# Memory update as a PSUM sum of its own, and long sums with 32-row shares from the first logits step on

## The chip, the cores and the metric

Every run used one core of a Trainium2 chip. The metric is device time in microseconds of one execution, taken from outside the profile. The profiled span (first to last instruction) is some 1.8 us shorter than the time of the same execution.

## The reference

`x` is 2048 x 1024. After a layer norm, two branches are added to the input:

```python
x = A_x
xn = _layernorm(x, axis=-1)
return x + _A_ref(xn, A_wq, A_wk, A_wv, A_wo, A_beta) + _B_ref(xn, B_w1, B_b1, B_w2, B_b2)

# A: 32 heads of 32, four segments of 512 tokens, causal inside a segment, and a memory over the segments
#    a_dot = softmax(q k' * scale + mask) v;  a_mem = (phi(q) M) / (phi(q) z + 1e-6)
#    o = g * a_mem + (1 - g) * a_dot;  then M += phi(k)' v, z += sum phi(k)
# B: token MLP: layer norm once more, gelu(h' w1 + b1) w2 + b2, with 2048 -> 3584 -> 2048 over the tokens
```

## The kernel before

The first MLP (h and w1) runs first, to about 200 us, and leaves `gT` (28 chunks of 128 rows). Everything else is interleaved after it by a list scheduler inside the program, which carries its own clock: attention is the fixed part, and the second MLP (`gT` times w2) with the output projection is "fill", put wherever attention would let TensorE wait. The scheduler is run when the program is built; on the chip the order is fixed.

Some words that come up often: PSUM is the memory that TensorE writes its results to, here in eight banks. A "sum" is a row of matmuls that add up in one bank. An "evacuation" is the copy by ScalarE or VectorE that empties a bank, after which the bank can be given to another sum. "Weighing" is the product of the softmax weights with v.

Attention comes in units (a group of four heads in one segment, 32 units). 46 logits steps feed them. A step has seven jobs in seven PSUM banks, of the eight: one 32-row group of TensorE has one job, the other three have two. So in the second half of a step one row group stands idle. A "long sum" of fill uses that: it leaves out its 28th chunk as a full matmul and does it as four shares of 32 rows, one in each of four steps.

```python
        def second(bs, some):                       # second half of a logits step
            if n >= fill.PLAIN and fill.L.sliced():
                fill.L.cut(rs)                      # the share, in row group rs, the one with a single job
            mms(bs, some)
```

The fill has two streams of weights, N (short sums, buffers `w2n`) and L (long sums, `w2l`, its share's slice in `w2s`):

```python
    PLAIN = 12                                      # the first 12 steps stand outside the scheme
    def __init__(self, k):
        rest = [(c, half, False, 0) for c in range(12, 16) for half in range(2)]
        long = []
        for j in range(3):
            g = [(c, half, True) for c in range(4 * j, 4 * j + 4) for half in range(2)]
            long += [x + (1,) for x in g[:3]]       # True: 8 matmuls of output projection in the same sum
            rest += [x + (0,) for x in g[3:]]
    ...
    def ready(self, t):                             # may the next logits step be placed?
        L, N, n = self.L, self.N, t.stage - 1
        if n < self.PLAIN:
            return N.open() and N.left() >= self.KEEP
        return L.i == self.want(n) and L.open() and not N.open()
```

The memory update sits in the last weighing of a unit and shares its bank:

```python
            if upd:                                 # in weigh(u, 3): pk' vA into columns of the same bank
                for c in range(4):
                    fw.mm(self.ps[:, b, 2 * GW:3 * GW], self.pk[u % 3][:, c, :],
                          vA[:, c, hl:hl + 4, :].rearrange("p h x -> p (h x)"), start=(c == 0), stop=(c == 3))
        ...                                         # ScalarE or VectorE: ost <- bank
        if upd:                                     # VectorE: memory <- bank, which only then is free
            fl.op({"dve": (lambda e, b: e.tensor_tensor(m32, m32, self.ps[:, b, 2 * GW:3 * GW], op=ALU.add), 283, 320)},
                  [R_o, self.R_MZ32[g]], [self.R_MZ32[g]], box=box, give=True, prio=0)
```

The softmax here doesn't subtract the row's maximum and nothing guards it: scores larger than these inputs give would overflow.

Of the kernel before, what the change touches and what calls it, by code (L numbers as in the profile page):

```python
# [7 lines left out]
ALU = mybir.AluOpType  # L8
# [7 lines left out]
N_SEG = 4  # L16
# [349 lines left out]
class _Flow:  # L366


    LOOK = 5
    MARGIN = 120  # L370
    MARGIN_STEP = 110
    PART = 160

# [61 lines left out]
    def next(self):  # L435
        fw, best = self.fw, None
        for t in self.avail:
            if t.gate is not None and not t.gate():
                continue
            reads = t.reads if t.box is None else t.reads + [self.R_bank[t.box["b"]]]  # L440
            r = fw.ready(reads, t.writes)
            for e, (fn, ns, busy) in t.engs.items():
                s = max(r, fw.now[e])
                key = (s, t.prio, t.n, s + ns)
                if best is None or key < best[0]:
                    best = (key, t, e, reads)
        return best
# [136 lines left out]
class _Kernel:  # L584
# [95 lines left out]
    def over_early(self):  # L680
# [5 lines left out]
        self.wkr = [e.take(f"wk{i}", [P, N_DCH, P], BF16) for i in range(2)]  # L686
        self.w2r = [e.take(f"w2n{i}", [P, 6, P], BF16) for i in range(4)]
        self.w2l = [e.take(f"w2l{i}", [P, 6, P], BF16) for i in range(3)]
        self.w2s = [e.take(f"w2s{i}", [P, P], BF16) for i in range(2)]
# [6 lines left out]
        self.R_wk = [Res(f"wk{i}", wait) for i in range(2)]  # L696
        self.R_w2 = [Res(f"w2n{i}", wait) for i in range(4)]
        self.R_w2l = [Res(f"w2l{i}", wait) for i in range(3)]
        self.R_w2s = [Res(f"w2s{i}", wait) for i in range(2)]
# [329 lines left out]
    def evac(self, dst, R_dst, box, view=lambda x: x):  # L1029
        self.flow.op({"act": (lambda e, b: e.activation(dst, view(self.bank(b)), ACT.Copy), 600, 540),  # L1030
                      "dve": (lambda e, b: e.tensor_copy(dst, view(self.bank(b))), 690, 727)},  # L1031
                     [], [R_dst], box=box, give=True, prio=0)
# [69 lines left out]
    def step(self, items):  # L1102
# [45 lines left out]
        for i, (r, blocks, slot, masks) in enumerate(items):  # L1148
            fl.op({"act": (lambda e, b, slot=slot: e.activation(pT[:, slot, :], self.bank(b), ACT.Exp, scale=SCALE),  # L1149
                           620, 488)}, [], [R[slot]], box=box[i], give=True)  # L1150
            v = pT[:, slot, :].rearrange("p (j q) -> p j q", q=P)
            if len(masks) > 1:
                ap, pat = v[:, masks[0]:masks[1] + 1:masks[1] - masks[0], :], [[0, 2], [1, P]]
            else:
                ap, pat = v[:, masks[0], :], [[1, P]]
            ns = 180 + 115 * len(masks)
            fl.op({"pool": (lambda e, ap=ap, pat=pat: e.affine_select(ap, ap, pattern=pat, compare_op=ALU.is_ge,  # L1157
                                                                      fill=0.0, base=0, channel_multiplier=-1),
                            ns, ns + 30)}, [R[slot]], [R[slot]])

    def weigh(self, u, qb):
# [5 lines left out]
        vA, R_vA = self.vA[i], self.R_vA[i]  # L1167
        upd = qb == 3 and s < N_SEG - 1
        where = {}
        for r in range(4):  # L1170
            for kb in range(qb + 1):
                slot, col = self.slot_of[u, r, kb]
                where[r, kb] = slot, col + (qb - kb) * P
        reads = [self.R_pT[slot] for slot in sorted({x[0] for x in where.values()})]
        reads += R_vA if upd else R_vA[0:qb + 1]
        if s:
            reads += [self.R_pqT[k], self.R_MZbf[g]]
        if upd:
            reads += [self.R_pk[u % 3]]

        def mms(b):
            fw = self.fw
            for r in range(4):
                for kb in range(qb + 1):
                    slot, col = where[r, kb]
                    fw.mm(self.ps[:, b, VW * r:VW * r + VW], self.pT[:, slot, col:col + P], vA[:, kb, hl + r, :],
                          start=(kb == 0), stop=(kb == qb))
            if s:
                fw.mm(self.ps[:, b, GW:2 * GW], self.pqT[k][:, qb * P:(qb + 1) * P], self.MZbf[:, g, :],
                      start=True, stop=True)  # L1190
            if upd:
                for c in range(4):
                    fw.mm(self.ps[:, b, 2 * GW:3 * GW], self.pk[u % 3][:, c, :],
                          vA[:, c, hl:hl + 4, :].rearrange("p h x -> p (h x)"), start=(c == 0), stop=(c == 3))

# [4 lines left out]
               "act": (lambda e, b: e.activation(dst, self.ps[:, b, 0:n * VW], ACT.Copy), 175 + n * 27, 140 + n * 27)},  # L1200
              [], [self.R_ost[o][qb]], box=box, give=not upd, prio=0)
        if upd:
            R_o = self.R_ost[o][qb]
            m32, mbf = self.MZ32[:, g, :], self.MZbf[:, g, :]
            dg = self.diag[:].rearrange("p r x -> p (r x)")
            if s == 0:
                fl.op({"dve": (lambda e, b: e.tensor_copy(m32, self.ps[:, b, 2 * GW:3 * GW]), 283, 320)},
                      [R_o], [self.R_MZ32[g]], box=box, give=True, prio=0)
            else:
                fl.op({"dve": (lambda e, b: e.tensor_tensor(m32, m32, self.ps[:, b, 2 * GW:3 * GW], op=ALU.add), 283, 320)},  # L1210
                      [R_o, self.R_MZ32[g]], [self.R_MZ32[g]], box=box, give=True, prio=0)
            fl.op({"dve": (lambda e: e.tensor_tensor(mbf, m32, dg, op=ALU.mult), 296, 330)},
                  [self.R_MZ32[g], self.R_diag], [self.R_MZbf[g]], prio=2)

# [44 lines left out]
    def attention_and_out(self):  # L1259
# [24 lines left out]
        for i, items in enumerate(steps):  # L1284
            fl.stage = i + 1
            self.step(items)
            while True:
# [4 lines left out]
                elif u < N_UNIT and last[u] <= i:  # L1292
                    self.proj_v(u)
                    for qb in range(4):
                        self.weigh(u, qb)
                    self.combine(u)
                    for slot in [x for x, us in self.users.items() if u in us]:
# [7 lines left out]
        goals = [0, 0]  # L1305
        knots = [(0, 0)] + [(last[8 * s + 7] + 2, 216 + 285 * s) for s in range(3)]
        knots += [(len(steps) - 1, self.fill.total - self.RESERVE), (len(steps), self.fill.total - 3)]
        for i in range(1, len(steps) + 1):
# [5 lines left out]
    def tail(self):  # L1314
# [37 lines left out]
        for x in pieces[5:]:  # L1352
            part(x, 0, 8)


# [117 lines left out]
class _Fill:  # L1473
    KEEP = 5
    PLAIN = 12
    SOON = 700

    def __init__(self, k):
        self.k = k
        self.closed = []  # L1480
        rest = [(c, half, False, 0) for c in range(12, 16) for half in range(2)]
        long = []
        for j in range(3):
# [3 lines left out]
        long[-1] = long[-1][:3] + (0,)  # L1487
        self.L = _Stream(k, self, long, "L", k.w2l, k.R_w2l, 2, [3])
        self.N = _Stream(k, self, rest, "N", k.w2r, k.R_w2, 3, [0, 1, 2])
        self.streams = [self.L, self.N]  # L1490
# [109 lines left out]
```

## Time and profile before

| | before |
|---|---|
| time, median of the runs beside the changed kernel | 692.03 us (691.76 to 692.76, 6 runs) |
| profiled span | 690.2 us |
| matmul records / weight loads | 4765 / 4846 |
| ScalarE, VectorE, GpSimd busy | 45%, 33%, 22% |

TensorE is the path, and the prediction shows by which lines. Two habits of reading are needed. Busy spans of matmuls overlap, so work is counted by start-to-start distances. And where matmul records are missing (81 here), the weight loads are complete and give the count.

I use one account for all kernels. A profile is split into the time to the first value projection (start and first MLP), the stretch from there to the start of the last matmul, and the end. The stretch is fixed work, counted matmul by matmul as in the prediction, and what is left of it: waits. Some 0.5 us of every figure for waits is reading error (46 steps by 0.01).

### The profile page before, as it was taken

To read this page: it belongs to the slowest core of one execution; us is meant where nothing else is said; L and a number is where in the kernel's file an instruction comes from. 1 tells how busy PE (TensorE), PEld (TensorE's weight loads), DVE (VectorE), ACT (ScalarE), POOL (GpSimd) and SP (SyncE) were. 2 spreads that over 40 slices of the span, in tenths; PEclk is the share of its full clock that TensorE was granted. 3 is DMA by queue.
4 is the path that set the end of the run, shared out by engine and by line. 5 is a ranking of instruction groups with operands and counts; after the bars stand their busy time and mean duration, and the time that the engine had idled before them with its cause. 6 is when DMAs were issued, how large, how long until landed. Compare 5 with 4: busy or idle time off the path is not lost.

```text
span 690.2 us, 11956 instructions
## 1 busy us (share of the span) xinstructions
PE 680.5 (99%) x4765; PEld 328.6 (48%) x4846; DVE 226.8 (33%) x500; ACT 313.5 (45%) x616; POOL 153.2 (22%) x379
## 2 busy tenths in 40 slices
PE   9999999999999999999999999999999999999998
PEld 3444444444444544544454444544545544454544
DVE  6731100000002323333453461633534534341524
ACT  7431111111136566564655462735754643644540
POOL 5820000000001233223223131312331331312330
PEclk9999999999999999999999999999999999999999
DMA  8367666325026558766556556465565456446334
GB/s 307 121 183 181 154 156 211 91 61 145 1 103 154 133 135 167 142 142 154 132 121 145 123 123 150 103 151 121 126 149 114 104 119 159 106 111 127 86 85 137
DMA packets 274960, 92.03 MB, mean 133 GB/s; under 512 B 233434, under 2 KB 271322, under 8 KB 274906
## 3 DMA queue, kind: packets, MB, share of 16 engines
q1 hardware_dynamic: 274906, 91.28, 54.1%
q8 instruction: 38, 0.62, 0.4%
q14 instruction: 16, 0.13, 0.1%
HBM read 74.47 MB, written 5.24 MB: 115 GB/s over the span
## 4 chain that ended last, share of the span: by engine, by line
PE 96%; issue 1%; ACT 1%; DMA 1%; POOL 0%; DVE 0%; SPq 0%; POOLq 0%; DVEq 0%
PE ps_all L217 96%; DMA xin<-in_A_x_dram 0%; DMA w2n<-in_B_w_dram 0%; ACT xn_tmp L851 0%; ACT xn_tmp L849 0%; POOL pT L1157 0%; DVE h L890 0%; POOL ln_r L882 0%; ACT pT L1149 0%; SPq L247 0%; DVE qT L1031 0%; POOLq L580 0%; DVE fin L1343 0%; POOL ln_t L880 0%; POOL ln_t L877 0%
## 5 line engine op out<-in xcount | busy, mean ns | idle before, releaser
L1157 POOL TENSOR_SCALAR_AFFINE_SELECT pT<-pT 128x256 bf16<-128x256 bf16 (+1 forms) x320 | 127.0, 405 | 506.8 <-ACT pT L1149 497.1
L217 PE MATMUL ps_all<-h,w1all 128*128 128x512 bf16 x878 | 192.9, 379 | 1.1
L1149 ACT ACTIVATE pT<-ps_all 128x512 bf16<-128x512 f32 x320 | 162.1, 620 | 48.9 <-PE ps_all L217 48.9
L217 PE MATMUL ps_all<-gT,w2n 128*128 128x512 bf16 x618 | 146.8, 379 | 2.2 <-issue 0.5
L217 PEld LDWEIGHTS ps_all<-h,w1all 128*128 128x128 bf16 x896 | 87.5, 98 | 106.3 <-DVE h L890 0.6
L1004 ACT ACTIVATE gT<-ps_all,bc 128x512 bf16<-128x512 f32 x56 | 37.7, 689 | 140.3 <-PE ps_all L217 134.8
L217 PEld LDWEIGHTS ps_all<-gT,w2n 128*128 128x128 bf16 x644 | 60.0, 98 | 69.6 <-issue 2.9
L1200 ACT ACTIVATE ost<-ps_all 128x264 bf16<-128x264 f32 (+1 forms) x99 | 35.0, 375 | 81.8 <-PE ps_all L217 81.0
L217 PE MATMUL ps_all<-xnT,wk 128*128 128x512 bf16 x255 | 60.4, 379 | 0.1
L1463 DVE SCALAR_TENSOR_TENSOR stg<-ps_all,bc,stg 128x512 bf16<-128x512 f32 x32 | 23.9, 747 | 110.7 <-PE ps_all L217 110.6
L217 PE MATMUL ps_all<-wv_sb,xnT 128*128 128x512 bf16 x254 | 59.9, 379 | 0.1
L217 PE MATMUL ps_all<-xnT,wq 128*128 128x512 bf16 x248 | 58.9, 379 | 0.4
L217 PE MATMUL ps_all<-gT,w2l 128*128 128x512 bf16 x226 | 57.8, 380 | 1.1 <-issue 0.5
L217 PEld LDWEIGHTS ps_all<-vA,pT 128*128 128x128 bf16 x1280 | 44.3, 96 | 14.2 <-POOL pT L1157 0.8
L1030 ACT ACTIVATE kT<-ps_all 128x512 bf16<-128x512 f32 x32 | 19.1, 597 | 60.6 <-PE ps_all L217 60.5
L217 PE MATMUL ps_all<-vA,pT 128*128 128x33 bf16 x1280 | 45.0, 177 | 0.5 <-POOL pT L1157 0.3
L217 PEld LDWEIGHTS ps_all<-wv_sb,xnT 128*128 128x128 bf16 x256 | 25.1, 98 | 30.2
L217 PEld LDWEIGHTS ps_all<-xnT,wk 128*128 128x128 bf16 x256 | 25.1, 98 | 30.2
L942 DVE TENSOR_SCALAR gcol<-gcol 128x32 f32<-128x32 f32 x1 | 0.2, 181 | 118.6 <-ACT gcol L940 118.6
L217 PEld LDWEIGHTS ps_all<-xnT,wq 128*128 128x128 bf16 x256 | 24.8, 98 | 29.0 <-issue 0.3
L217 PEld LDWEIGHTS ps_all<-gT,w2l 128*128 128x128 bf16 x244 | 21.3, 98 | 25.1 <-issue 5.8
L1015 DVE TENSOR_SCALAR etmp<-etmp 128x512 bf16<-128x512 bf16 x48 | 14.1, 293 | 55.1 <-ACT etmp L1014 55.1
(74 smaller groups left out, 489.2 us busy)
## 6 DMA issues: line engine op xcount, KB each, us to landing
w2n<-in_B_w_dram SPq DMA_DIRECT2D x92, 192.0 KB, 2.8
w1all<-in_B_w_dram SPq DMA_DIRECT2D x12, 1024.0 KB, 5.3
wq<-in_A_wq_dram SPq DMA_DIRECT2D x32, 256.0 KB, 2.8
wk<-in_A_wk_dram SPq DMA_DIRECT2D x32, 256.0 KB, 3.2
w2l<-in_B_w_dram SPq DMA_DIRECT2D x36, 192.0 KB, 2.9
stg<-in_A_x_dram SPq DMA_DIRECT2D x32, 128.0 KB, 3.3
out_dram<-stg SPq DMA_DIRECT2D x32, 128.0 KB, 2.0
w2n<-in_B_w_dram SPq DMA_DIRECT2D x23, 128.0 KB, 2.5
```

Of the source, the lines that this page charges most:

```text
L217: ins = self.nc.tensor.matmul(out, *args, **kwargs)
L942: fw.op("dve", lambda e: e.tensor_scalar(self.gcol[:], self.gcol[:], 1.0, None, op0=ALU.add), reads=[self.R_gcol], writes=[self.R_gcol])
L1004: fw.op("act", lambda e: e.activation(self.gT[:, fc, half * 512:(half + 1) * 512], self.bank(b), ACT.Gelu_apprx_tanh, bias=self.b1c[:, fc: ...
L1015: fl.op({"dve": (lambda e: e.tensor_scalar(et[:], et[:], 1.0, None, op0=ALU.min), 294, 330)}, [R_et], [R_et], prio=2)
L1030: self.flow.op({"act": (lambda e, b: e.activation(dst, view(self.bank(b)), ACT.Copy), 600, 540), "dve": (lambda e, b: e.tensor_copy(dst, v ...
L1149: fl.op({"act": (lambda e, b, slot=slot: e.activation(pT[:, slot, :], self.bank(b), ACT.Exp, scale=SCALE), 620, 488)}, [], [R[slot]], box= ...
L1157: fl.op({"pool": (lambda e, ap=ap, pat=pat: e.affine_select(ap, ap, pattern=pat, compare_op=ALU.is_ge, fill=0.0, base=0, channel_multiplie ...
L1200: "act": (lambda e, b: e.activation(dst, self.ps[:, b, 0:n * VW], ACT.Copy), 175 + n * 27, 140 + n * 27)},
L1463: engs={"dve": (lambda e, b: e.scalar_tensor_tensor(dst, k.bank(b), k.b2c[:, c:c + 1], dst, op0=ALU.add, op1=ALU.add), 750, 785)},
```

## The change

Its intent: let three more long sums carry shares, so that all steps from the first take one; free the last weighing of a unit from the memory update; and adapt weight buffers and scheduler constants to that. Of the constants, MARGIN and MARGIN_STEP are the time by which the plan stays behind the moment when the data and banks of the next attention matmuls, or of a logits step, should be ready; PART is how long before its last bank is free a step may start; SPM is added to the planned start of a DMA transfer. The diff, cut to its core:

```diff
-    MARGIN = 120
-    MARGIN_STEP = 110
-    PART = 160
+    MARGIN = 50
+    SPM = 300
+    MARGIN_STEP = 60
+    PART = 200
@@ next(): the plan's start of an operation
-                s = max(r, fw.now[e])
+                s = max(r + (self.SPM if e == "sp" else 0), fw.now[e])
@@ weight buffers (ring depths go with them: 3 -> 4 and 2 -> 3)
-        self.w2r = [e.take(f"w2n{i}", [P, 6, P], BF16) for i in range(4)]
-        self.w2l = [e.take(f"w2l{i}", [P, 6, P], BF16) for i in range(3)]
+        self.w2r = [e.take(f"w2n{i}", [P, 5, P], BF16) for i in range(5)]
+        self.w2l = [e.take(f"w2l{i}", [P, 4, P], BF16) for i in range(4)]
@@ step(): assumed time of a mask (and 620 -> 575 for an exponential, 600 -> 585 for an evacuation)
-            ns = 180 + 115 * len(masks)
+            ns = 225 + 115 * len(masks)
@@ a new function; the same lines go out of weigh()
+    def memory(self, u):
+        def mms(b):
+            for c in range(4):
+                self.fw.mm(self.ps[:, b, 0:GW], self.pk[u % 3][:, c, :], ...)
+        box = fl.pe(mms, R_vA + [self.R_pk[u % 3]])[0]
+        ...                                         # VectorE adds it into the memory, and gives the bank back
@@ order of a unit
+                    if upd:
+                        self.memory(u)
                     for qb in range(4):
                         self.weigh(u, qb)
+                    if upd:
+                        self.spread(u)
@@ how much fill by the end of each segment
-        knots = [(0, 0)] + [(last[8 * s + 7] + 2, 216 + 285 * s) for s in range(3)]
+        knots = [(0, 0)] + [(last[8 * s + 7] + 2, 206 + 285 * s) for s in range(3)]
@@ _Fill
-    PLAIN = 12
+    PLAIN = 0
-        long = []
+        n = (12 - self.PLAIN) // 4
+        long, rest = [x[:3] + (1,) for x in rest[:n]], rest[n:]
```

More of the change, by code (lines that the diff above doesn't have):

```diff
@@ L696, in over_early @@
         self.R_wk = [Res(f"wk{i}", wait) for i in range(2)]
-        self.R_w2 = [Res(f"w2n{i}", wait) for i in range(4)]
-        self.R_w2l = [Res(f"w2l{i}", wait) for i in range(3)]
+        self.R_w2 = [Res(f"w2n{i}", wait) for i in range(5)]
+        self.R_w2l = [Res(f"w2l{i}", wait) for i in range(4)]
         self.R_w2s = [Res(f"w2s{i}", wait) for i in range(2)]
@@ L1029, in evac @@
     def evac(self, dst, R_dst, box, view=lambda x: x):
-        self.flow.op({"act": (lambda e, b: e.activation(dst, view(self.bank(b)), ACT.Copy), 600, 540),
+        self.flow.op({"act": (lambda e, b: e.activation(dst, view(self.bank(b)), ACT.Copy), 585, 540),
                       "dve": (lambda e, b: e.tensor_copy(dst, view(self.bank(b))), 690, 727)},
@@ L1149, in step @@
             fl.op({"act": (lambda e, b, slot=slot: e.activation(pT[:, slot, :], self.bank(b), ACT.Exp, scale=SCALE),
-                           620, 488)}, [], [R[slot]], box=box[i], give=True)
+                           575, 488)}, [], [R[slot]], box=box[i], give=True)
             v = pT[:, slot, :].rearrange("p (j q) -> p j q", q=P)
@@ L1159, in step, with spread @@
                             ns, ns + 30)}, [R[slot]], [R[slot]])
+    def memory(self, u):
+        fl = self.flow
+        s, g = u // N_GRP, u % N_GRP
+        hl = 4 * (g % 4)
+        vA, R_vA = self.vA[(u // 4) % 2], self.R_vA[(u // 4) % 2]
+        def mms(b):
+            for c in range(4):
+                self.fw.mm(self.ps[:, b, 0:GW], self.pk[u % 3][:, c, :],
+                           vA[:, c, hl:hl + 4, :].rearrange("p h x -> p (h x)"), start=(c == 0), stop=(c == 3))
+        box = fl.pe(mms, R_vA + [self.R_pk[u % 3]])[0]
+        m32 = self.MZ32[:, g, :]
+        if s == 0:
+            fl.op({"dve": (lambda e, b: e.tensor_copy(m32, self.ps[:, b, 0:GW]), 283, 320)},
+                  [], [self.R_MZ32[g]], box=box, give=True, prio=0)
+        else:
+            fl.op({"dve": (lambda e, b: e.tensor_tensor(m32, m32, self.ps[:, b, 0:GW], op=ALU.add), 283, 320)},
+                  [self.R_MZ32[g]], [self.R_MZ32[g]], box=box, give=True, prio=0)
+    def spread(self, u):
+        g = u % N_GRP
+        mbf, m32 = self.MZbf[:, g, :], self.MZ32[:, g, :]
+        dg = self.diag[:].rearrange("p r x -> p (r x)")
+        self.flow.op({"dve": (lambda e: e.tensor_tensor(mbf, m32, dg, op=ALU.mult), 296, 330)},
+                     [self.R_MZ32[g], self.R_diag], [self.R_MZbf[g]], prio=2)
     def weigh(self, u, qb):
@@ L1167, in weigh @@
         vA, R_vA = self.vA[i], self.R_vA[i]
-        upd = qb == 3 and s < N_SEG - 1
         where = {}
@@ L1173, in weigh @@
                 where[r, kb] = slot, col + (qb - kb) * P
-        reads = [self.R_pT[slot] for slot in sorted({x[0] for x in where.values()})]
-        reads += R_vA if upd else R_vA[0:qb + 1]
+        reads = [self.R_pT[slot] for slot in sorted({x[0] for x in where.values()})] + R_vA[0:qb + 1]
         if s:
             reads += [self.R_pqT[k], self.R_MZbf[g]]
-        if upd:
-            reads += [self.R_pk[u % 3]]
         def mms(b):
@@ L1190, in mms @@
                       start=True, stop=True)
-            if upd:
-                for c in range(4):
-                    fw.mm(self.ps[:, b, 2 * GW:3 * GW], self.pk[u % 3][:, c, :],
-                          vA[:, c, hl:hl + 4, :].rearrange("p h x -> p (h x)"), start=(c == 0), stop=(c == 3))
         box = fl.pe(mms, reads)[0]
@@ L1200, in weigh @@
                "act": (lambda e, b: e.activation(dst, self.ps[:, b, 0:n * VW], ACT.Copy), 175 + n * 27, 140 + n * 27)},
-              [], [self.R_ost[o][qb]], box=box, give=not upd, prio=0)
-        if upd:
-            R_o = self.R_ost[o][qb]
-            m32, mbf = self.MZ32[:, g, :], self.MZbf[:, g, :]
-            dg = self.diag[:].rearrange("p r x -> p (r x)")
-            if s == 0:
-                fl.op({"dve": (lambda e, b: e.tensor_copy(m32, self.ps[:, b, 2 * GW:3 * GW]), 283, 320)},
-                      [R_o], [self.R_MZ32[g]], box=box, give=True, prio=0)
-            else:
-                fl.op({"dve": (lambda e, b: e.tensor_tensor(m32, m32, self.ps[:, b, 2 * GW:3 * GW], op=ALU.add), 283, 320)},
-                      [R_o, self.R_MZ32[g]], [self.R_MZ32[g]], box=box, give=True, prio=0)
-            fl.op({"dve": (lambda e: e.tensor_tensor(mbf, m32, dg, op=ALU.mult), 296, 330)},
-                  [self.R_MZ32[g], self.R_diag], [self.R_MZbf[g]], prio=2)
+              [], [self.R_ost[o][qb]], box=box, give=True, prio=0)
     def combine(self, u):
@@ L1293, in attention_and_out @@
                     self.proj_v(u)
+                    upd = u // N_GRP < N_SEG - 1
+                    if upd:
+                        self.memory(u)
                     for qb in range(4):
                         self.weigh(u, qb)
+                    if upd:
+                        self.spread(u)
                     self.combine(u)
@@ L1305, in attention_and_out @@
         goals = [0, 0]
-        knots = [(0, 0)] + [(last[8 * s + 7] + 2, 216 + 285 * s) for s in range(3)]
-        knots += [(len(steps) - 1, self.fill.total - self.RESERVE), (len(steps), self.fill.total - 3)]
+        knots = [(0, 0)] + [(last[8 * s + 7] + 2, 206 + 285 * s) for s in range(3)]
+        knots += [(len(steps) - 1, self.fill.total - 60), (len(steps), self.fill.total - 3)]
         for i in range(1, len(steps) + 1):
@@ L1487, in __init__ @@
         long[-1] = long[-1][:3] + (0,)
-        self.L = _Stream(k, self, long, "L", k.w2l, k.R_w2l, 2, [3])
-        self.N = _Stream(k, self, rest, "N", k.w2r, k.R_w2, 3, [0, 1, 2])
+        self.L = _Stream(k, self, long, "L", k.w2l, k.R_w2l, 3, [3])
+        self.N = _Stream(k, self, rest, "N", k.w2r, k.R_w2, 4, [0, 1, 2])
         self.streams = [self.L, self.N]
```

## The prediction

> **What bounds the kernel now.** I read first the page's busy times and its chain of work that ended last:
>
> ```profile
> PE 680.5 (99%) x4765; PEld 328.6 (48%) x4846; DVE 226.8 (33%) x500; ACT 313.5 (45%) x616; POOL 153.2 (22%) x379
> ...
> PE 96%; issue 1%; ACT 1%; DMA 1%; POOL 0%; DVE 0%; SPq 0%; POOLq 0%; DVEq 0%
> ```
>
> TensorE is busy 680.5 of 690.2 us and holds 96% of the chain; VectorE, ScalarE and GpSimd are below half. But busy time alone does not say how much of it could still go, so the waits of TensorE came next:
>
> ```profile
> PE ps_all L217 <- DVE gT L800: 1.3, 1, 1.3
> PE ps_all L217 <- issue: 1.1, 7, 0.2
> PE ps_all L217 <- DMA w2n<-in_B_w_dram: 0.4, 1, 0.4
> PE ps_all L217 <- POOL pT L1157: 0.3, 1, 0.3
> ```
>
> (Columns: total us, times, longest.) The 1.3 is the start, before the first weights are there. The seven "issue" waits of 0.16 us each are gaps before which a matmul record is missing: the page has 4846 weight loads and only 4765 matmuls, each of which has one load. What is left are two real waits, 0.4 and 0.3.
>
> Busy spans overlap, so I counted the work by start-to-start distances instead. In the timeline of TensorE the 128x512 matmuls start 215.8 ns apart in long runs, the 33-column weighing matmuls 25.4 ns, the 132-column ones 56.8 ns. The logits steps are these (start, length, then the group):
>
> ```profile
> 309.53 0.38 PE L217 MATMUL ps_all<-gT,w2n 128*128 128x512 bf16 x1
> 309.85 0.61 PE L217 MATMUL ps_all<-qT,kT 32*128 32x512 bf16 x10
> 310.39 0.39 PE L217 MATMUL ps_all<-gT,w2n 128*128 128x512 bf16 x1
> ```
>
> A step without a share takes 310.39 - 309.85 = 0.54 us, and its first matmul starts 0.32 us after the last full one instead of 0.216, so 0.64 us in all. The same with a share (w2s) in it:
>
> ```profile
> 328.80 0.55 PE L217 MATMUL ps_all<-qT,kT 32*128 32x512 bf16 x7
> 329.03 0.37 PE L217 MATMUL ps_all<-gT,w2s 32*128 32x512 bf16 x1
> 329.04 0.37 PE L217 MATMUL ps_all<-qT,kT 32*128 32x512 bf16 x3
> 329.34 0.60 PE L217 MATMUL ps_all<-gT,w2l 128*128 128x512 bf16 x2
> ```
>
> Again 329.34 - 328.80 = 0.54 us: the share is free. This pair of readings carries the prediction.
>
> The sum: 2800 full matmuls (896 first MLP, 888 second, 768 q/k/v, 248 output) x 0.2158 = 604.2; 16 halves of the last output tile 1.7; 1280 x 0.0254 = 32.5; 192 x 0.0568 = 10.9; 46 logits steps x 0.642 = 29.5. Together 678.9 us. From the first MLP matmul (6.56) to the start of the last matmul (687.56) there are 681.0. So only some 2.1 us of that stretch is not fixed work. Taken step by step, by counting weight loads between two logits steps, they lie in three places: 0.5 in the first microseconds of the first MLP (the layer norm feeds it), 0.6 near 582 us, 0.5 after 668 us, and about 0.5 as 0.01 to 0.02 per step, which is reading error. The two later ones in the timeline, first of the DMA queue:
>
> ```profile
> 576.99 2.30 SPq L247 DMA_TRANSPOSE xnT<-o_s  x1
> 579.33 1.17 SPq L247 DMA_DIRECT2D w2n<-in_B_w_dram  x2
> ```
>
> and, of TensorE,
>
> ```profile
> 582.13 2.33 PE L217 MATMUL ps_all<-gT,w2n 128*128 128x512 bf16 x9 [0.38 <-DMA w2n<-in_B_w_dram]
> ...
> 671.48 0.27 PE L217 MATMUL ps_all<-vA,pT 128*128 128x33 bf16 x4 [0.32 <-POOL pT L1157]
> ```
>
> The first: the DMA queue's program sits 2.3 us in one transpose (its siblings take about 1.2), the two weight transfers behind it go late, and TensorE waits. The second: after the last logits step the fill work is nearly used up, and the weighing waits for the last masks.
>
> **What the Trainium skill says.** "TensorE: Matmul & The Clock Gate", Back-to-back issue gap: warm spacing is N/2.4 + 2.5 ns, 215.8 at 512 columns; the trace agrees (215.8). The same page, Part 3 (The mechanism): matmuls in different 32-row groups run at the same time, starting about 4 ns apart; the trace agrees (2 to 5 ns between starts of logits matmuls of one width) and shows the share riding along. "TensorEngine Tiling (Array Packing)", Key Properties: a change of the tiling mode drains the engine; the trace fits (312 ns before a step's first matmul where 216 is usual), and the change removes none of these switches. "DMA: Bandwidth & Descriptors", Anatomy of one DMA, gives about 2 us of fixed time per transfer (for another issuing path); here a 192 KB weight piece lands after a median of 2.8 us and a 128 KB one after 2.5, so smaller pieces do not land in proportion sooner.
>
> **The change part by part.**
>
> *More long sums with shares.* Twelve steps stood outside the scheme before (PLAIN 12); the long stream had nine sums, eight of them with a 27-chunk sum plus four shares. Now PLAIN is 0, three further sums join, eleven have shares: 11 x 4 = 44 shares, steps 0 to 43. Removed: 3 full matmuls of 0.2158 = 0.65 us. Added: 12 shares of 32 rows, at 0 us each by the pair above. Weight loads go from 4846 to 4846 - 3 + 12 = 4855. Gain 0.65 us, directly on the path, since TensorE is the path.
>
> *Memory update as its own sum.* The same 96 matmuls of 132 columns (5.5 us), the same 24 additions (292 to 295 ns on VectorE) and 24 spreads. TensorE's work does not change. What changes: the last weighing of a unit no longer waits for the transposed pk, its evacuation gives its bank back at once, and the addition no longer waits for the evacuation (in the reading of the memory tile, VectorE sat idle 23.1 us over 22 such waits for ScalarE's weighing evacuation). But VectorE is 33% busy and no wait of TensorE names a weighing bank, so this frees time that nobody used. It needs 24 more bank allocations, with the logits steps wanting seven banks. Gain 0.
>
> *Smaller weight pieces, more of them.* Short stream: 23 sums x 5 pieces = 115 become 20 x 6 = 120, five buffers of five chunks. Long stream: 45 become 12 x 7 = 84, four of four. With the three added slices, 47 more transfers. The lead of the short stream goes from 3 x 6 = 18 to 4 x 5 = 20 matmuls, 3.9 to 4.3 us, against 2.5 to 3.6 us to landing. Five of the 115 pieces now land just when TensorE takes them, and one pair makes the 0.6 us wait; 0.4 us more lead covers part of that. The long stream's lead stays 12 matmuls, and there the tightest piece landed 3.1 us early.
>
> *Scheduler constants.* SPM 300 puts a transfer that is chosen by the scheduler into the DMA queue's order only 0.3 us after its data should be ready, which takes the blocking transposes out of the weight pieces' way. That is the second remedy for 582 us. The margins shrink (120 to 50, 110 to 60 ns): matmuls are placed closer to when their data comes, which invites waits of tens of ns, 46 steps long. The mask's assumed time grows by 45 ns, towards the measured mean of 405 to 410 for the double masks, and this may take some of the 0.3 us at 671. The startup and the last 2.5 us after the last matmul are untouched.
>
> *Sum.* -0.65 (shares), -0.4 (I give 70% to the 0.6 us of the late transfer going), -0.1 (end), +0.2 (new small waits): -0.95 us. 692.19 - 0.95 = 691.2.
>
> **Rivals.**
>
> 1. *The new schedule waits more.* Every constant of a greedy scheduler moved, so the whole order of 440 us changes, and a single late transfer costs 0.5 us. For it: smaller margins, 47 more transfers in one queue, one more bank user. Against: long leads on the long stream, a median of 6 us early on the short one, engines at half load. Two or three such waits eat the gain: 692.0 to 693.
> 2. *All real waits go.* Then -0.65 - 0.6 - 0.5 = 1.75: 690.4. For it: both remedies aim at the known wait. Against: the wait at the end comes from the fill work having run out, and the reserve of 60 is unchanged.
> 3. *The shares are not free in the early steps*, because the first sums need their slices early or the stricter order (a long sum must be open and no short one) stalls a step. Then the 0.65 is lost: about 692. Against: the first slices are loaded long before the first step at 215 us, and the same rule held from step 12 on without a wait.
> 4. *The separate sum delays the logits for want of a bank*: 24 x 0.1 us would make 693.5 or more. Against: the bank is held for some 0.3 us of VectorE and the joint one before was held for both evacuations in turn.
>
> **Range and chances.** Fixed work allows no more than about 1.75 us; 690.3 is the low end, below rival 2 by spread of the runs (0.9 us between the three). The high end, 692.5, leaves room for two new waits against the full gain of the shares. Faster by over 2% would need 678.3 us, below the fixed work plus start and end: 0.5%. Slower by over 2% needs 13.8 us of waits, a broken schedule: 1%. Within 2%: 98.5%.
>
> **What would show it.** Right: weight loads 4855, of them 44 with the 32-row slice; every logits step still 0.54 us, with a share or not; no wait of TensorE for w2n near the old place; memory additions that start before or beside the last weighing's evacuation; end of the last matmul some 1 us earlier. Wrong: waits of TensorE on w2n, w2l, pk or vA that total over 1 us, logits steps of 0.6 us or more, or a first step later than 215.2 us. The prediction fails most likely in the small terms: the shares' 0.65 is counted, the net of -0.3 for waits is a judgment.

## More of the kernel before

The experiments ran on two chips (e3, e4, e5 and e7 on one, the others on the other), each call with the kernel before beside it, so times of different calls are compared by their ratios to it.

## The result, and the profile after

691.17 us (690.88 to 692.29, 6 runs) against 692.03. The ratio of the two is 0.9989, with a 95% interval of 0.9976 to 1.0002: within 2%, and by the runs alone not even surely below one. The gain in the medians is 0.86 us, where 0.95 was predicted. Ratios here are the mean time of one kernel's fast runs over that of the other's in the same rounds, so not quite the ratio of the medians that I quote.

The page of the changed kernel, its busy line and its chain:

```profile
PE 685.0 (99%) x4855; PEld 327.3 (47%) x4855; DVE 234.8 (34%) x505; ACT 309.6 (45%) x611; POOL 153.9 (22%) x379
...
PE 97%; ACT 1%; DMA 1%; POOL 0%; DVE 0%; SPq 0%; issue 0%; POOLq 0%; DVEq 0%
```

4855 weight loads, as counted. TensorE's busy time rose by 4.5 us while the kernel got faster: no matmul record is missing here, 81 were before. This is why the busy time is of no use for such a difference. Its waits (total us, times, longest):

```profile
PE ps_all L217 <- DVE gT L801: 1.3, 1, 1.3
PE ps_all L217 <- POOL pT L1158: 0.3, 1, 0.3
PE ps_all L217 <- DVE h L891: 0.2, 1, 0.2
```

The wait for `w2n` is gone, the one for the masks at the end is still there. A step with a share in the timeline of TensorE (start, length, group):

```profile
327.87 0.55 PE L217 MATMUL ps_all<-qT,kT 32*128 32x512 bf16 x7
328.10 0.38 PE L217 MATMUL ps_all<-gT,w2s 32*128 32x512 bf16 x1
328.11 0.37 PE L217 MATMUL ps_all<-qT,kT 32*128 32x512 bf16 x3
328.41 0.60 PE L217 MATMUL ps_all<-gT,w2l 128*128 128x512 bf16 x2
```

328.41 - 327.87 = 0.54 us, as before. The account of the two profiles, in us:

| | start and first MLP | fixed work | waits | end | span |
|---|---|---|---|---|---|
| before | 200.44 | 485.48 | 1.64 | 2.69 | 690.25 |
| after | 200.66 | 484.84 | 1.16 | 2.68 | 689.33 |

So 0.64 us of the gain in the profile is fixed work (three matmuls of 0.216), 0.48 is waits (0.54 for `w2n` went, 0.14 after step 7 is new), and 0.2 is lost again in the first microseconds, where the kernels do not differ and the profiles scatter from 200.44 to 200.92.

The total was as predicted to 0.03 us. With an interval of 0.9 us to each side, so close an agreement is luck, and whether its terms were right, a total that agrees does not show. Hence the experiments.

### The profile page after: what moved, and what is told of

Same layout as the page of the kernel before. It is cut to its first block, busy times and chain, and to the rows that moved or that the text cites. A ratio compares the mean times of both kernels' runs of the same rounds, so it can differ in the third digit from the quotient of the medians.

```text
span 689.3 us, 12154 instructions
## 1 busy us (share of the span) xinstructions
PE 685.0 (99%) x4855; PEld 327.3 (47%) x4855; DVE 234.8 (34%) x505; ACT 309.6 (45%) x611; POOL 153.9 (22%) x379
## 4 chain that ended last, share of the span: by engine, by line
PE 97%; ACT 1%; DMA 1%; POOL 0%; DVE 0%; SPq 0%; issue 0%; POOLq 0%; DVEq 0%
PE ps_all L217 97%; DMA xin<-in_A_x_dram 1%; ACT xn_tmp L850 0%; POOL pT L1158 0%; DVE h L891 0%; SPq L247 0%; ACT xn_tmp L852 0%; ACT pT L1150 0%; POOL ln_r L883 0%; POOLq L581 0%; DVE fin L1356 0%; POOL ln_t L881 0%; DVE ln_mv L866 0%; DVEq L65 0%
## 5 line engine op out<-in xcount | busy, mean ns | idle before, releaser
L217 PE MATMUL ps_all<-gT,w2n 128*128 128x512 bf16 x560 | 124.1, 379 | 0.0
L217 PE MATMUL ps_all<-gT,w2l 128*128 128x512 bf16 x325 | 86.0, 380 | 0.0
L217 PEld LDWEIGHTS ps_all<-gT,w2n 128*128 128x128 bf16 x560 | 54.4, 98 | 64.0 <-DMA w2n<-in_B_w_dram 0.2
L217 PE MATMUL ps_all<-xnT,wq 128*128 128x512 bf16 x256 | 60.4, 379 | 0.0
L217 PEld LDWEIGHTS ps_all<-vA,pT 128*128 128x128 bf16 x1280 | 41.2, 96 | 5.5 <-POOL pT L1158 1.0
L217 PEld LDWEIGHTS ps_all<-gT,w2l 128*128 128x128 bf16 x325 | 27.6, 97 | 33.7 <-issue 10.1
L217 PE MATMUL ps_all<-vA,pT 128*128 128x33 bf16 x1280 | 42.8, 177 | 0.3 <-POOL pT L1158 0.3
L217 PEld LDWEIGHTS ps_all<-xnT,wq 128*128 128x128 bf16 x256 | 23.4, 97 | 29.5 <-issue 6.4
L217 PE MATMUL ps_all<-wo_sb,oT 128*128 128x512 bf16 x128 | 31.2, 379 | 0.0
```

The source lines that it names most:

```text
L217: ins = self.nc.tensor.matmul(out, *args, **kwargs)
```

## The experiments

The theory: the shares give their 0.65 us by themselves, the separate memory sum gives nothing, and the lost wait for weights is due to the queue order or the lead. The rivals are in the expectations. All results were correct. Accounts first, explanations after:

| run | time (median, us) | ratio to before | fixed work | waits | span |
|---|---|---|---|---|---|
| before + early shares only (e1) | 694.28 | 1.0025 | 484.84 | 4.94 | 693.34 |
| after, early shares undone (e2) | 692.50 | 1.0001 | 485.49 | 1.43 | 690.74 |
| after, memory joint again (e3) | 693.23 | 1.0014 | 484.83 | 3.37 | 691.80 |
| before + SPM only (e4) | 692.42 | 1.0008 | 485.47 | 2.60 | 691.29 |
| before + weight buffers only (e5) | 692.50 | 1.0007 | 485.50 | 0.98 | 690.42 |
| after, share in a busy row group (e6) | 700.65 | 1.0118 | 484.85 | 10.84 | 698.99 |
| after, SPM 0 (e7) | 691.39 | 0.9991 | 484.83 | 1.24 | 689.29 |
| after, longer last masks in the plan (e8) | 691.31 | 0.9983 | 484.83 | 1.90 | 690.16 |
| joint memory + long sum held back (e9) | 692.77 | 1.0011 | 484.82 | 2.97 | 690.94 |
| after, old margins (e10) | 692.50 | 1.0006 | 484.85 | 2.72 | 690.77 |
| after + held back + last masks (e11) | 690.48 | 0.9980 | 484.84 | 0.68 | 688.70 |
| e11 + more lead for short sums (e12) | 691.75 | 0.9998 | 484.84 | 2.25 | 690.65 |

The intervals of the ratios are about 0.0013 wide to each side, 0.9 us. So differences under a microsecond are read from the accounts, which rest on one profile for each kernel, and those of the times are only told. The 10.84 of e6 contain the longer steps that it was made to test, 44 times 0.216, or 9.5.

### The shares alone, on the kernel before

```diff
-    PLAIN = 12
+    PLAIN = 0
+        n = (12 - self.PLAIN) // 4
+        long, rest = [x[:3] + (1,) for x in rest[:n]], rest[n:]
```

> The kernel before with nothing changed but three more long sums with shares, from the first logits step on. Theory (the shares ride along in the short row group, and TensorE is the path): 4855 weight loads, fixed work 0.65 us less, every logits step still 0.54 us from its first matmul to the next full one, so 0.65 us less than the kernel before (about 691.4 us), give or take the waits of the new order (at most 0.6 us each way; the one for a short-stream weight piece may move or stay). Rival (the gain of the whole change came from the transfers and the scheduler alone): the time of the kernel before, 692.0, with the same waits in the profile.

694.28 us (693.77 to 695.07) against 692.37 of the kernel before in the same rounds, ratio 1.0025 (1.0012 to 1.0039): slower. The fixed work fell by the predicted 0.64, but the waits grew by 3.3. Both theory and rival missed this. Here is the eighth step, step 7, in the timeline of TensorE of this run:

```profile
278.63 0.40 PE L217 MATMUL ps_all<-qT,kT 32*128 32x512 bf16 x7
279.17 0.39 PE L217 MATMUL ps_all<-gT,w2s 32*128 32x512 bf16 x1
279.17 0.39 PE L217 MATMUL ps_all<-qT,kT 32*128 32x512 bf16 x3
279.50 0.39 PE L217 MATMUL ps_all<-gT,w2l 128*128 128x512 bf16 x1
280.31 1.90 PE L217 MATMUL ps_all<-wv_sb,xnT 128*128 128x512 bf16 x8 [0.43 <-ACT pT L1149]
```

After the step TensorE has one long-sum matmul to do, then waits for an exponential to give a PSUM bank back, since the step took seven of eight and the open sum has the eighth. Between the two halves of the step, too, it came late (279.17 - 278.63 = 0.54, where 0.23 is usual); the trace names ScalarE's evacuation of kT, which holds a bank. In the changed kernel the same step is followed by two long-sum matmuls, and loses 0.14 us. At step 3 the second half waits for something else, VectorE's memory instruction (MZ), which empties the bank that the memory update shares with the last weighing:

```profile
247.43 0.39 PE L217 MATMUL ps_all<-qT,kT 32*128 32x384 bf16 x5
248.07 0.37 PE L217 MATMUL ps_all<-gT,w2s 32*128 32x512 bf16 x1 [0.25 <-DVE MZ L1207]
```

I counted the long-sum matmuls that follow each of the first twelve steps in the compiled order (e3 and e10 are told below):

| after step | 0 to 2 | 3 | 4 to 6 | 7 | 8 to 10 | 11 |
|---|---|---|---|---|---|---|
| after | 3, 3, 3 | 3 | 3, 3, 3 | 2 | 3, 3, 3 | 3 |
| e1 | 4, 4, 4 | 1 | 4, 4, 4 | 1 | 4, 4, 5 | 1 |
| e3 | 3, 3, 3 | 1 | 3, 3, 3 | 1 | 3, 3, 3 | 1 |
| e10 | 4, 4, 4 | 1 | 4, 4, 4 | 1 | 4, 4, 4 | 1 |

Where the table shows 1, at every fourth step, where the sum takes its fourth share, these kernels wait: by start-to-start distances 2.5 us in all three places of e1, 1.5 in those of e3 and 1.5 in those of e10. Elsewhere are waits of 0.9 for `w2n` and 0.24 for a mask in e1, of 0.43 at step 23, 0.40 for a mask and 0.38 for `w2n` in e3, and of 0.24 for `w2n` in e10. The reason is in the diff: an early long sum has 27 full matmuls for four steps, where a later one has 27 and 8 of the output projection. The plan of the kernel before takes four or five before a step and four after it, 32 or more in four steps. In e1, 35 are enough for that and 27 are not. And while a step is near, no short sum may be open, so there is nothing else to take.

### The early shares undone in the changed kernel

```diff
-    PLAIN = 0
+    PLAIN = 12
```

> The changed kernel with the first twelve steps outside the scheme again (eight sums with shares, 4846 weight loads); all else stays. Theory: 0.65 us more than the changed kernel, about 691.8, still without a wait on the weight pieces. Rival: no difference to the changed kernel, 691.2.

692.50 (691.95 to 692.89), ratio 1.0001 (0.9989 to 1.0014); fixed work 485.49. The counted 0.65 us is back. Waits are 0.27 more (one of 0.37 for `w2n`, against 0.14 after step 7), and the end took 0.5 more (the last output write was issued later and landed in 1.9 us instead of 1.5). So in the changed plan the shares are a gain, in the plan before they were a loss.

### The memory update put back

The edit restores the joint form in `weigh` and takes out `memory` and `spread`.

> The changed kernel with the memory update put back into the last weighing of each unit; shares, weight pieces and constants stay. Theory (the separate sum frees only idle time of VectorE): within 0.3 us of the changed kernel, about 691.2, and VectorE's additions wait for ScalarE's evacuations again. Rival (the separate sum is what lets the banks and the steps flow): slower by 0.5 us or more, with waits of TensorE for banks or for vA and pk before the steps.

693.23 (692.75 to 693.53), ratio 1.0014 (1.0001 to 1.0028): 1.7 us more than the changed kernel by the ratios, 2.2 by the waits of the account (of which 0.38 is a late `w2n` piece, the kind of wait that comes and goes). The rival had it right. The waits of TensorE in this run, of those on banks and masks:

```profile
PE ps_all L217 <- ACT pT L1150: 1.2, 4, 0.5
...
PE ps_all L217 <- POOL pT L1158: 0.6, 2, 0.3
```

The way into step 3 shows why. First TensorE in the changed kernel's timeline:

```profile
244.43 0.39 PE L217 MATMUL ps_all<-vA,pk 128*128 128x132 bf16 x4
244.66 1.18 PE L217 MATMUL ps_all<-vA,pT 128*128 128x33 bf16 x40
245.68 0.81 PE L217 MATMUL ps_all<-gT,w2l 128*128 128x512 bf16 x3
246.42 0.40 PE L217 MATMUL ps_all<-qT,kT 32*128 32x384 bf16 x5
```

and in this run's, to the wait after the step:

```profile
245.13 1.17 PE L217 MATMUL ps_all<-vA,pT 128*128 128x33 bf16 x40
246.15 0.39 PE L217 MATMUL ps_all<-vA,pk 128*128 128x132 bf16 x4
246.59 0.81 PE L217 MATMUL ps_all<-gT,w2l 128*128 128x512 bf16 x3
247.33 0.40 PE L217 MATMUL ps_all<-qT,kT 32*128 32x384 bf16 x5
...
247.88 0.39 PE L217 MATMUL ps_all<-gT,w2l 128*128 128x512 bf16 x1
248.52 0.59 PE L217 MATMUL ps_all<-xnT,wq 128*128 128x512 bf16 x2 [0.26 <-ACT pT L1150]
```

With a sum of its own, the memory update comes ahead of the weighing, and its bank is long free when the step needs it. Joined, it comes last, and its bank is emptied twice in turn, by ScalarE to 246.85 and by VectorE to 247.18, in the timeline of VectorE:

```profile
246.88 0.30 DVE L1208 COPY MZ<-ps_all 128x132 f32<-128x132 f32 x1 [0.77 <-ACT ost L1201]
```

The plan covers that with long-sum matmuls, four before the step against three in the changed kernel (82 matmul records are missing in this run, one of them here; the weight loads show all four), and then has only one left after the step, where the wait comes: 0.26 of idle time by the view, which models the ends of matmuls, and 0.43 from start to start.

```profile
246.32 0.59 PEld L217 LDWEIGHTS ps_all<-gT,w2l 128*128 128x128 bf16 x4
```

### The joint form, with the long sum held back

```diff
-        if self.at == self.size() - 1 and cut and self.cuts < 4:
+        if self.at >= self.size() - 4 and cut and self.cuts < 4:
```

> The changed kernel with the joint memory update (2 us slower than the changed kernel) and one more rule: the last four matmuls of a long sum with shares are kept until its fourth share is in. Theory (the early long sums have only 27 matmuls of their own for four steps, and the joint order spends them before the fourth step, so that TensorE then has nothing to do until the exponentials give a bank back): the three waits of 0.4 to 0.8 us after steps 3, 7 and 11 go, about 691.7. Rival (the joint sum holds its bank too long, whatever the order): the waits stay or move ahead of the step, 693 or more.

692.77 (692.74 to 692.85), ratio 1.0011. The waits after the steps went, three or four matmuls now follow each, but waits of 0.43, 0.54, 0.32 and 0.53 us stand inside steps 3, 7, 11 and 23. My theory, that only the placing was wrong, fell; the rival's "move ahead of the step" came near. Step 3 of this run:

```profile
245.69 0.39 PE L217 MATMUL ps_all<-vA,pk 128*128 128x132 bf16 x4
245.91 0.38 PE L217 MATMUL ps_all<-gT,w2l 128*128 128x512 bf16 x1
246.22 0.40 PE L217 MATMUL ps_all<-qT,kT 32*128 32x384 bf16 x5
246.87 0.37 PE L217 MATMUL ps_all<-gT,w2s 32*128 32x512 bf16 x1 [0.25 <-DVE MZ L1208]
```

Now the second half of the step waits for the bank of the joint sum itself. So at step 3 both are true at once: the sum is too short to cover the banks on both sides of the fourth step, and the joint form makes the side before it longer. At steps 7 and 11 the bank waited for was that of kT, and at step 23 the trace names another instruction of VectorE; there the separate form's help, if it is that, is indirect, through the whole order.

### The old margins in the changed kernel

```diff
-    MARGIN = 50
-    MARGIN_STEP = 60
+    MARGIN = 120
+    MARGIN_STEP = 110
```

> The changed kernel with the two margins of the kernel before (120 and 110 ns). The plan then takes four long-sum matmuls after a step where it took three, so the early sums are down to one after every fourth step. Theory (27 matmuls last four steps only with three after each): waits of TensorE for a bank of the exponentials after steps 3, 7 and 11, 1.5 to 2 us in all, about 693. Rival (the separate memory sum alone makes the early shares possible, the margins are fine tuning): about 691.2, no waits over 0.2 us.

692.50 (692.16 to 692.69), ratio 1.0006 (0.9992 to 1.0019). The waits after steps 3, 7 and 11 are 0.43, 0.49 and 0.54, 1.5 in all, as expected. The margin is added to the time at which a bank should be ready, so with 120 ns the plan takes a fourth matmul where a third would do. So in these profiles the shares from the first step on need both: the separate memory sum and the small margins.

### A share in a busy row group

```diff
-                fill.L.cut(rs)
+                fill.L.cut((rs + 1) % 4)
```

> The changed kernel with each share moved to the next row group, one that has two logits matmuls in the step instead of one; results stay right, since over four steps each quarter still comes once. Theory (a share costs nothing only because its row group would stand idle): each of the 44 steps with a share grows by one 512-column pass, 0.216 us, to 0.76 us; sum 9.5 us, about 700.7. Rival (row groups are fed in such a way that a 32-row matmul is hidden anywhere, or the steps wait for their banks anyway): about 691.2, steps of 0.54 us.

700.65 (700.03 to 700.77) against an expected 700.7. In this run's timeline, the step shown of the changed kernel above now takes 331.19 - 330.43 = 0.76 us:

```profile
330.43 0.55 PE L217 MATMUL ps_all<-qT,kT 32*128 32x512 bf16 x7
330.66 0.37 PE L217 MATMUL ps_all<-gT,w2s 32*128 32x512 bf16 x1
330.81 0.44 PE L217 MATMUL ps_all<-qT,kT 32*128 32x128 bf16 x3
331.19 0.39 PE L217 MATMUL ps_all<-gT,w2l 128*128 128x512 bf16 x1
```

All 44 steps with a share took 0.75 or 0.76 us. So a share is free where its row group stands idle; in a busy one it costs a whole pass of 0.216 us.

### Queue order and weight buffers

SPM alone on the kernel before, the buffers alone on it, and SPM at zero in the changed kernel:

> The kernel before with nothing changed but the 300 ns that a transfer chosen by the scheduler is held back in the plan. Theory (the 0.6 us at 582 is a queue whose program stood in a transpose that came too early): the transposes that stood over 2 us are gone, the wait for the weight piece with them, 0.5 us less than the kernel before, 691.5. Rival (the lead of the short stream is too small by itself): the wait stays or moves, 692.0.

> The kernel before with nothing changed but the weight buffers: five of five chunks and four of four instead of four and three of six. Theory (two matmuls more of lead on the short stream help in part): the wait for a weight piece goes or falls below 0.2 us, fewer than five pieces land just when they are taken, about 691.5. Rival (the queue's order does it, lead does not): the wait stays, 692.0, or grows with the 47 to 40 added transfers.

> The changed kernel without the 300 ns for transfers. Theory (queue order): waits of TensorE for a weight piece come back, 0.3 to 0.6 us, about 691.6. Rival (lead): no such wait, 691.2, though the queue's program stands longer in its transposes.

With SPM alone TensorE waited more for `w2n`, not less, and no time was gained (692.42, ratio 1.0008). From its waits (total us, times, longest):

```profile
PE ps_all L217 <- DMA w2n<-in_B_w_dram: 1.1, 3, 0.4
```

Nor were the transposes that stand over 2 us in the queue's program gone: there are nine, where the kernel before has six. The theory fell. With the buffers alone (e5) the wait was gone from the profile, and with SPM at zero (e7) it did not return (691.39, ratio 0.9991 against 0.9989). So nothing here speaks for the queue order, and the profiles point to the lead. But they do not show it. e5's time did not fall (692.50, ratio 1.0007): in its profile the end took 0.5 us more, as in e2, and the start 0.3. And e8, whose order is that of the changed kernel up to 666 us, waited 0.8 us for a `w2n` piece that the changed kernel's profile did not wait for. This wait depends on the run: the piece was issued 0.7 us later than in the changed kernel and took 4.4 us to land instead of 3.4. e6, with the same order of transfers, waited 0.4. One profile can neither show it cured nor not.

### The last masks in the plan, and the version that puts things together

```diff
-            ns = 225 + 115 * len(masks)
+            ns = 225 + 115 * len(masks) + (110 if len(items) == 5 else 0)
```

> The changed kernel with 110 ns more assumed for each of the five masks of the last logits step, so that two more fill matmuls are placed ahead of the last weighing. No operation is added or taken away. Theory (the 0.5 us lost after the last step is a wait of TensorE for masks that the plan thought ready, with fill work left over behind it): the wait on the mask goes or falls to 0.1, about 0.4 us less than the changed kernel, 690.8. Rival (the last weighing sets the end through the transpose of its result, so what is put ahead of it comes back at the end): 691.2, with a wait later in the last output sums.

The place behaved as expected: the wait after the last step, 0.48 to 0.49 from start to start in every kernel without this edit, is 0.05. The account does not show it, since this profile, of the slowest of the five runs (691.89), has the late weight piece; by the ratios (0.9983 against 0.9989) e8 is 0.4 us ahead of the changed kernel, as expected, but within the scatter. The wait itself, as I read it, comes from GpSimd's masks running beside VectorE's multiplications of the unit before. The masks of the last step in the changed kernel's timeline (start, length, group):

```profile
667.20 2.82 POOL L1158 TENSOR_SCALAR_AFFINE_SELECT pT<-pT 128x256 bf16<-128x256 bf16 x5 [7.94 <-ACT pT L1150]
```

and VectorE in the same stretch:

```profile
667.31 0.83 DVE L1253 TENSOR_TENSOR o_s<-ost,srec 128x512 bf16<-128x512 bf16 x1
668.07 0.89 DVE L1253 TENSOR_TENSOR prod<-ost,srec 128x512 bf16<-128x512 bf16 x1
```

One by one in the trace, the masks took 0.41, 0.73, 0.85, 0.47 and 0.40 us (the fourth is a smaller one, 128x128), and the multiplications 0.83 and 0.89, where the next unit's took 0.69 and 0.68. The whole trace of the changed kernel has the same pattern: 128x256 masks took 0.41 at the median (163 of them) when neither these multiplications nor the addition after them ran at the same time, and 0.59 (29) when one did for over 0.1 us; 128x128 masks took 0.29 (113) and 0.50 (15), and the second multiplication 0.68 (11) without a mask beside it and 0.89 (13) with one. By these medians, as an estimate, the last five masks would take 0.9 us less undisturbed, more than the wait. The plan knows nothing of it. The Trainium skill has a reason on its page "SBUF — State Buffer", section "SBUF: two separate sides": a VectorE instruction with two inputs in SBUF and a GpSimd instruction that reads SBUF need the same pair of ports, and the one that starts first holds it to its end while the other blocks. The durations here fit that, if blocked time counts in them. No experiment moved the masks away to prove it.

The held-back rule and this repair together, on the changed kernel (e11), and then with six short-stream buffers of five chunks and four long-stream buffers of three chunks (e12):

> The changed kernel with two small repairs: the last four matmuls of a long sum kept until its fourth share, and 110 ns more assumed for each mask of the last step. Theory: the waits of 0.15 us after step 7 and of 0.5 after the last step go; 0.5 us less than the changed kernel, about 690.7 where the weight pieces land in time. Rival: no difference beyond the scatter, 691.2, because a late weight piece takes what is won.

> The kernel of the run with the two repairs, with six short-stream buffers of five chunks (lead 25 matmuls instead of 20) and long-stream buffers of three chunks instead of four (lead 9). Theory (the waits for a weight piece that come in one run and not in another are a lead that is too short for the slowest landings): no short-stream piece lands within 0.3 us of its use, no wait on w2n, the lowest and the tightest times of this study, about 690.4. Rival (the long stream's lead becomes the short one): waits on w2l, 691 or more.

e11 took 690.48 us (690.43 to 690.86) against 691.99 of the kernel before in the same rounds, ratio 0.9980 (0.9967 to 0.9992). The only line among its waits of TensorE (the view lists idle times over 0.15 us) is the one at the start:

```profile
PE ps_all L217 <- DVE gT L801: 1.3, 1, 1.3
```

It is the best version of this study: against the kernel before the gain is clear of the scatter, against the changed kernel (another call, ratio 0.9989) it is 0.6 us by the ratios and 0.5 in the waits of the account, which is plausible and not proved by the times.

e12 was 1.3 us slower than e11 (691.75). Its short-stream half worked: no `w2n` piece landed less than 1.85 us before its use, where the changed kernel has one just in time (0.04). But it took the long stream's lead from 12 matmuls to 9, and at the end that is what TensorE waits for, in the timeline:

```profile
670.37 0.82 PE L217 MATMUL ps_all<-gT,w2l 128*128 128x512 bf16 x3 [1.46 <-DMA w2l<-in_B_w_dram]
```

## Why the prediction was right or wrong

The number was right, and so was the term that carried it. Several of the small terms had the wrong reasons, and that they still added up was luck.

- *Fixed work, -0.65.* Right: 485.48 to 484.84, 4855 weight loads, steps of 0.54 us, and e6 shows why a share costs nothing.
- *Memory update, "Gain 0".* Wrong. In the changed kernel it is worth some 1.7 us by the ratios (e3). The step that failed: "this frees time that nobody used", because "no wait of TensorE names a weighing bank". That was read from a kernel in which fill covered every such wait. The early long sums take that cover away, and then the same bank is on the path (step 3 of e1 and of e9). What was predicted of VectorE came true: its idle time before the memory instructions fell from 23.1 us in 22 waits to 2.6 in 8.
- *Rival 3, that the early shares stall a step, argued away with "the same rule held from step 12 on without a wait".* This happened in e1 in full: waits 3.3 us up. What I missed is that the sums from step 12 on have 35 matmuls and the early ones 27; both numbers stood in the code.
- *Smaller margins, "+0.2".* A new small wait came (0.14 after step 7), but as the effect of the margins the sign is wrong. They are what makes 27 matmuls last four steps (e10: 1.56 us more waits with the old ones).
- *Weight pieces, -0.4.* The size came out in the profile (0.54 went), the split did not: SPM, the "second remedy", does nothing that could be seen (e4, e7). The lead helps in the profiles of e5 and e12, but the wait comes and goes between runs. The "2.5 to 3.6 us to landing" was too narrow a reading: these pieces took 2.1 to 4.9 us in the kernel before, and the new lead of 4.3 does not cover the slowest.
- *End, -0.1.* The wait stayed at 0.49. The 45 ns that I counted on were too few beside masks of 0.73 and 0.85 us. And the 405 to 410 was misread: it is the mean of all masks, while the double ones alone have a mean of 450 and a median of 406 in the kernel before.
- *Two smaller readings.* The wait of 1.3 at the start is not for weights: the line names VectorE, which clears the operand of 14 warm-up matmuls. And of the signs of being wrong, one came up without meaning: the first step began at 215.43, later than 215.2, but 14.77 us after the first value projection, as in the kernel before (14.78).

So what the change is made of: a counted gain of 0.65 us, and a group of other parts most of which are there to keep that gain from being lost in waits. Undone one by one, two of them look like gains of 1 to 2 us (e3, e10); two others, added to the kernel before, gave no time that could be seen (e4, e5). Open: whether the memory sum or the margins alone, without the shares, would help the kernel before; that was not run. PART, the fill goal of 206 and the new assumed times were not tried by themselves either. By what path the separate sum also removes the waits for kT at steps 7 and 11 is not settled either.

## What to carry to other kernels

Where idle time is covered by filler work, a profile of the covered kernel cannot tell which waits are harmless: before moving filler, count how much of it each place needs and how much it will have. Here that was 27 against 32, a count that needs no chip. And test a change of several parts both ways, a part alone and the whole without it: the shares cost 1.7 us alone and gained 0.8 in company, by the ratios (the 0.8 is within the scatter; the counted part of it is 0.65).

## What the Trainium skill lacked or had wrong

- "TensorEngine Tiling (Array Packing)", Key Properties, says that a change of mode drains the engine and gives no time. Here the first matmul of a logits step starts 312 ns after a full one instead of 216.
- "TensorE: Matmul & The Clock Gate", Back-to-back issue gap, gives about 131 ns a matmul for a sustained stream of weight load and matmul at 512 columns, and 216 as the isolated gap. Here 215.8 ns is the sustained distance with a weight load for each of 2800 matmuls, and nothing came near 131. At 132 columns a pair of load and matmul takes 56.8 ns, where it gives 81 for 128 columns. Its Part 3 has no case in which a tile's row group is already taken: here that cost 0.22 us a step at 512 columns (e6), a whole pass.
- No page tells how far the landing of one and the same transfer scatters from run to run: short-stream pieces of the changed kernel took 2.7 us at the median and 4.3 at most, and one that took 3.4 there took 4.4 in e8. With the later issue of that piece, kernels with the same order of transfers waited 0 to 0.8 us.
